# Sparse attention and an MLP on one core: the first batch's prologue rewritten (masks as a bias matmul, local q and k on the upper partitions, filler products)

## The chip, the cores and the metric

The kernel runs on one core of a Trainium2 chip. The metric is the device time of one launch in microseconds; lower is better. A core has five engines with a queue of instructions each: PE (TensorE, matmuls and transposes), DVE (VectorE), ACT (ScalarE), POOL (GpSimd) and SP (SyncE, which here only issues transfers). Transfers issued by SP and ACT go through hardware queues (q1 and q10 in the profile), those issued by POOL through a software queue (q0); all run on the same 16 DMA engines.

## The reference

```python
def _attn_ref(q, k, v):                    # (8, 8, 576, 64) float32 each
    scores = matmul(q, k.transpose(0, 1, 3, 2)) / sqrt(64)
    rel = pos[:, None] - pos[None, :]
    mask_local = (rel >= 0) & (rel < 32)                                  # heads 0 to 3
    mask_strided = (rel >= 0) & (pos[None, :] % 32 == pos[:, None] % 32)  # heads 4 to 7
    scores = where(mask, scores, -1e9)
    return matmul(softmax(scores), v)

def reference(q, k, v, moe_w_in, moe_w_out):
    x = attn_out.transpose(0, 2, 1, 3).reshape(4608, 512)
    h = x @ w_in                            # (512, 2048)
    return (h * tanh(softplus(h))) @ w_out  # (2048, 512)
```

## The kernel before

The work is cut into the 8 batches of the attention (576 tokens each) and 9 tiles of 512 tokens of the MLP. While the MLP runs on tile t, the attention of batch t+1 is woven between its matmuls, and the loads of batch t+2 and later are issued. The order on every engine is the order in which the program issues instructions (a manual schedule); waits are set where an instruction needs another engine's or a transfer's result, or a buffer that is still read.

Attention works on two kinds of heads. For the local heads ("l"), six windows of 96 queries look at 128 keys each. For the strided heads ("s"), the tokens are regrouped so that a unit is a block of 72 queries and 72 keys. `qk` makes products of qT and kT into one of three accumulators in PSUM (`acc(0..2)`, two banks each) and lets ACT write the exponential to `P_s` or `P_l`. `mask` multiplies these by a matrix of zeros and ones on DVE (L289). `pv` and `pv2` multiply by v, with a column of ones that gives the sum, and DVE divides (L316, L317, or L330, L331 for two windows at once). `xt` transposes the result into `xT`, which the MLP reads. qT and kT come from PE transposes with the identity `ident` for batches 0 and 1, and from DMA transposes for batches 2 and later (L172 for s, L180 for l), which SP issues after POOL or DVE has cast the loaded float32 to bf16.

The MLP's first half `mlp1` is 8 groups of 8 matmuls of 128x512 (L428), each two columns of 128 of w_in, and ACT applies Mish (L433). For tile 0 the first two groups are split, so that channels 256 to 511 (the s heads) come first. The second half `mlp2` is 16 groups of 4 matmuls (L467), for tile 0 with w_out's quarters in the outer loop; the next batch's attention steps are placed between these groups (`attn_steps`).

Batch 0 has no MLP to be woven into. Its prologue is written out by hand from L483 on:

- SP issues four loads of k and q of the s heads into `st0` (L493), then v of the s and l heads (L115, L126, L129), then batch 1's local k and q (L104).
- POOL clears `P_l` (L504), issues two casting loads of batch 0's local k and q into `lq0` (L506, on partitions 0 to 95 with 6 tokens each), clears rows 64 to 79 of ks and qs of batch 1 (L534), and copies four numbers of vs (`held`, L535): that copy does nothing but hold the loads of w_in behind it (L136, five pieces) until vs is cast. One cast of vl stands between the third and the fourth piece. Then follow the loads of batch 1's ks and qs (L97) and of the first two quarters of w_out (L142).
- DVE casts ks and qs from `st0` in four steps (L151); PE transposes them (L207), ACT and DVE copy the transposes out of PSUM. The three s parts of `qk` follow, then DVE's masks and the cast of vs, then `t_step_loc0` for local k and q (L236), with `pv2` between, and so on up to `xt` of the local heads and the MLP.

After the prologue, a load of a few bytes of w_in (`gate`, L559) stands in SP's queue: it waits for the fifth piece of w_in, and all SP's later loads (batch 1's v, batch 2's k, q and v) stand behind it. In the same way `rest_of_w_out` holds POOL's loads of w_out's second half behind a copy from batch 1's kTl (L579). SP then issues, in this order: v of batch 1, local k and q of batch 2, vs of batch 2, the DMA transposes of ks and qs of batch 2, vl of batch 2, two stores of the output, and four DMA transposes of local k and q of batch 2.

Of the kernel before, what the change touches and what calls it, by code (L numbers as in the profile page):

```python
# [10 lines left out]
F32 = mybir.dt.float32  # L11
# [6 lines left out]
WQ = 96  # L18
CL, PL = 6, 96
SU = 80  # L20
CS, PN = 8, 72
RING = 4


def _consts():

    kk = np.arange(128)[:, None]
    qq = np.arange(WQ)[None, :]
    rel = qq + 32 - kk
    p = np.arange(PN)  # L30
    c = np.zeros((128, 128 + WQ + PN), np.float32)
    c[:, 0:128] = np.eye(128)
    c[:, 128:128 + WQ] = (rel >= 0) & (rel < STRIDE)
    c[:PN, 128 + WQ:] = (p[:, None] % 4 == p[None, :] % 4) & (p[:, None] <= p[None, :])
    return c.astype(ml_dtypes.bfloat16)


# [1 line left out]
def kernel(ctx, tc, q, k, v, moe_w_in, moe_w_out, out):  # L39
# [12 lines left out]
    w_in = const.tile([128, 4, DF], BF16, name="w_in")  # L52
    w_out = const.tile([128, 16, DM], BF16, name="w_out")
    xT = const.tile([128, 4, RT], BF16, name="xT")
    consts = const.tile([128, 128 + WQ + PN], BF16, name="consts_sb")
    ident = consts[:, 0:128]
    loc = consts[:, 128:128 + WQ]
    stm = consts[0:PN, 128 + WQ:128 + WQ + PN]
    vl32 = const.tile([128, 4, NW, D], F32, name="vl32")
    vs32 = const.tile([128, 4, CS, D], F32, name="vs32")  # L60
    ql32 = const.tile([128, 4, CL, D], F32, name="ql32")
# [11 lines left out]
    P_s = [const.tile([PN, 2, n * PN + 56], BF16, name=f"Ps{i}") for i, n in enumerate((6, 6, 4))]  # L73
    P_l = [const.tile([128, 2, n * WQ + 32], BF16, name=f"Pl{i}") for i, n in enumerate((5, 5, 2))]
    gate = const.tile([1, 256], BF16, name="gate")
    held = const.tile([1, 4], BF16, name="held")
    x_l = const.tile([128, NW, 256], BF16, name="x_l")
    x_s = const.tile([128, CS, 256], BF16, name="x_s")

# [7 lines left out]
    def acc(i, name):  # L87

        return ps_a.tile([128, 2, 512], F32, tag=f"acc{i}", name=name)
# [50 lines left out]
    def load_w_out(c0, c1):  # L140
        for c in range(c0, c1):
            nc.gpsimd.dma_start(  # L142
                w_out[:, 4 * c:4 * c + 4, :],
                moe_w_out.rearrange("(fc p) o -> p fc o", p=128)[:, 4 * c:4 * c + 4, :],
            )

    def cast(eng, out_, in_):
        if eng is nc.scalar:
# [82 lines left out]
    def t_step_loc0(src, dst, hp, eng):  # L231

        tr = tile_t("tr")[:].bitcast(BF16)
        for j in range(CL):
            for e in range(2):
                nc.tensor.transpose(  # L236
                    tr[64 * e:64 * e + 64, PL * j:PL * j + PL], src[0:PL, 2 * hp + e, j, :],
                    ident[0:PL, 0:PL],
                )
        cast(  # L240
            eng, dst.rearrange("c (p j) -> c p j", j=CL),
            tr[:, 0:S].rearrange("c (j p) -> c p j", j=CL),
        )

    T_ORDER = [(kd, w, hp) for kd in ("s", "l") for hp in range(2) for w in ("k", "q")]

# [12 lines left out]
    class Attn:  # L259
        def __init__(self, b):  # L260
            self.b = b

        def qk(self, parts, i_acc):

            ps, o = acc(i_acc, "ps"), 0
            todo = []
            for kind, i in parts:
                w = WQ if kind == "l" else PN
                o0 = o
                for x, y in PARTS[kind][i]:  # L270
                    for e in range(2):
                        r = slice(64 * e, 64 * e + 64)
                        if kind == "l":
                            lhsT, rhs = kTl[r, y, WQ * x:WQ * x + 128], qTl[r, y, WQ * x:WQ * x + WQ]
                        else:
                            c0 = SU * (4 * y + x)
                            lhsT, rhs = kTs[r, c0:c0 + 128], qTs[r, c0:c0 + PN]
                        nc.tensor.matmul(ps[:, e, o:o + w], lhsT=lhsT, rhs=rhs, start=True, stop=True)  # L278
                    o += w
                todo.append((kind, i, o0, o - o0))  # L280
            for kind, i, o0, nw in todo:
                n, pt = (128, P_l[i]) if kind == "l" else (PN, P_s[i])
                nc.scalar.activation(pt[0:n, :, 0:nw], ps[0:n, :, o0:o0 + nw], AF.Exp, scale=scale)  # L283
# [199 lines left out]

    with tc.manual_schedule():
        Po, Dv, Sc = nc.gpsimd, nc.vector, nc.scalar
        Sc.preload_act_table(AF.Exp)
        Sc.dma_start(consts[:], consts_h.ap())
        st0 = g_pool.tile([128, 16, 512], BF16, tag="gT", name="st0")
# [9 lines left out]
        load_v_loc(0)  # L498
        load_qk_loc(1)
        lq0 = g_pool.tile([128, 16, 512], BF16, tag="gT", name="lq0")  # L500
        lq0 = lq0[:].rearrange("p a b -> p (a b)")[0:PL]
        kl0, ql0 = [lq0[:, 1536 * i:1536 * i + 1536].rearrange("p (h x) -> p h x", h=4) for i in range(2)]
        for p in P_l:
            Po.memset(p[:], 0.0)  # L504
        for dst, src in ((kl0, k), (ql0, q)):
            Po.dma_start(dst, src[0, 0:4].rearrange("h (p j) d -> p h (j d)", j=CL))  # L506
        kl0, ql0 = [x.rearrange("p h (j d) -> p h j d", d=D) for x in (kl0, ql0)]
        Dv.memset(kTs[:], 0.0)
        Dv.memset(kTl[:, :, 0:32], 0.0)
# [7 lines left out]
            Dv.memset(p[:], 0.0)  # L517

        a = Attn(0)
        for hp in range(2):  # L520
            h = 2 * hp
            cast(Dv, ks[0][0:PN, h:h + 2, :], st0[0][:, h:h + 2, :])
            t_step(0, "s", "k", hp, Sc)
        for hp in range(2):
            h = 2 * hp
            cast(Dv, qs[0][0:PN, h:h + 2, :], st0[1][:, h:h + 2, :])
            t_step(0, "s", "q", hp, Dv if hp else Sc)
        for i in range(3):
            a.qk([("s", i)], i)
        a.mask("s", 0, Dv)  # L530
        cast(Dv, vs[0][0:PN, :, :, 0:D], vs32[0:PN])
        a.mask("s", 1, Dv)
        for x in (ks, qs):
            Po.memset(x[1][64:SU], 0.0)  # L534
        Po.tensor_copy(held[:], vs[0][0:1, 3, 0, 0:4])  # L535
        load_w_in(0, 256)
        load_w_in(256, 512)
        load_w_in(512, 1024)
        cast_v_loc(0, Po, 0, 3)
        load_w_in(1024, 1536)  # L540
        load_w_in(1536, 2048)
        for hp in range(2):
            t_step_loc0(kl0, kTl[:, hp, 32:32 + S], hp, Sc)
        a.pv2("s", 0, 0)
        a.mask("s", 2, Dv)
        a.pv2("s", 2, 1)
        for hp in range(2):
            t_step_loc0(ql0, qTl[:, hp, :], hp, Sc)
        a.qk([("l", 0)], 2)
        a.pv2("s", 4, 0)  # L550
        a.qk([("l", 1)], 1)
        a.mask("l", 0, Dv)
        a.pv2("s", 6, 0)
        cast_v_loc(0, Sc, 3, 6)
        a.qk([("l", 2)], 2)
        a.mask("l", 1, Dv)
        load_qk_str(1)
        load_w_out(0, 2)
        nc.sync.dma_start(gate[:], w_in[0:1, 0, 1536:1792])  # L559
        load_v(1)  # L560
        accs = (2, 1, 0)
        gT, g1 = mlp1(0, accs)
        a.xt("s", 0)
        a.xt("s", 1)
        Sc.preload_act_table(AF.Mish)
        a.pv2("l", 0, 1)
        a.mask("l", 2, Dv)
        a.pv2("l", 2, 0)
        a.pv("l", 4)
        a.pv("l", 5)  # L570
        a.xt("l", 0)
        a.xt("l", 1)
        cast_qk_loc(1, Po, Po)
        for x in (ks, qs):
            Po.memset(x[0][64:SU], 0.0)
        load_qk_loc(2)

        def rest_of_w_out():
            Po.tensor_copy(held[:], kTl[0:1, 1, 32:36])  # L579
            load_w_out(2, 4)  # L580
            load_qk_str(2)
            cast_qk_loc(2, Po, Po)
# [78 lines left out]
```

The softmax here doesn't subtract the row's maximum and nothing guards it: scores larger than these inputs give would overflow.

## Time and profile before

| what | value |
|---|---|
| median of 4 runs | 321.33 us (320.7 to 323.05) |
| the profiled execution | 322.08 us, of which the span is 320.3 us |
| PE, busy in the span | 301.4 us (94%) |
| ACT / DVE / POOL, busy in the span | 172.7 / 128.0 / 42.0 us |
| granted clock of PE, mean | 1.00 |
| bytes moved | 46.72 MB, 146 GB/s over the span |
| mean DMA engine busy share, first slices of 8 us | 6, then 9 (tenths) to about 200 us |
| first MLP matmul (L428) | 26.48 us |
| first matmul with w_out (L467) | 44.12 us |

All times within the profile count from the span's start. The span is from the first to the last instruction of the profiled execution; the time of that execution is 1.8 us longer. A line of the timeline gives the start, the time to the end of the last instruction of a merged group, the engine, the line of the program, the operation and its tiles; in brackets stands how long the engine was idle just before it, and what ended that. A line of the waits gives the engine, the waiting operation, what it waited for, the total in microseconds, how often, and the longest. A line of the chain gives the start, the length and what the end of the program hung on at that time. A line of a queue gives its packets, its megabytes and the time of its packets as a share of 16 engines' time; shares of several queues add up to more than 100% where packets overlap. The duration of a transfer issue on SP is how long SP was held by it, not how long the transfer took.

### The profile page before, as it was taken

Reading aid. Unit: us, or ns where it says so; the run is one execution under the profiler, and the core shown is the slowest. Engines: PE = TensorE matmul, PEld = TensorE weight load, DVE = VectorE, ACT = ScalarE, POOL = GpSimd, SP = SyncE. Lnnn points to the kernel's source line nnn. Section 1 sums busy time; section 2 is a strip of 40 time slices with the busy share of each in tenths; the row PEclk is TensorE's granted clock in tenths of the full one; section 3 lists DMA queues with packets and bytes.
Section 4 is the critical chain, followed back from the end, with each engine's and each line's share of the span. In section 5 each row is a group of like instructions: output and inputs, shape, how many; then the busy total and the mean of one; then the engine's idle time right before and its main releaser. Section 6 shows DMA issues by size and latency. Waiting matters only on the chain.

```text
span 320.3 us, 5867 instructions
## 1 busy us (share of the span) xinstructions
PE 301.4 (94%) x2488; PEld 159.7 (50%) x2488; DVE 128.0 (40%) x332; ACT 172.7 (54%) x195; POOL 42.0 (13%) x50
## 2 busy tenths in 40 slices
PE   0678999899899999999999999999999999999995
PEld 0564455444454445544578555445544554444444
DVE  6672067800477038703880288028801830000000
ACT  2572654386637673757475646664666466315601
POOL 9288030245000100200020000000000000000000
PEclk9999999999999999999999999999999999999999
DMA  6999999999999999899979995895540101011012
GB/s 172 217 229 206 222 203 188 177 194 227 178 185 216 171 189 211 195 140 184 223 140 172 184 207 115 159 197 137 96 100 0 68 22 46 0 65 65 2 56 75
DMA packets 103114, 46.72 MB, mean 146 GB/s; under 512 B 85168, under 2 KB 95728, under 8 KB 103088
## 3 DMA queue, kind: packets, MB, share of 16 engines
q1 hardware_dynamic: 91648, 37.22, 64.3%
q0 software_dynamic: 11152, 8.92, 18.5%
q8 instruction: 19, 0.31, 0.4%
q10 hardware_dynamic: 288, 0.21, 0.2%
q14 instruction: 7, 0.06, 0.1%
HBM read 38.34 MB, written 9.44 MB: 149 GB/s over the span
## 4 chain that ended last, share of the span: by engine, by line
PE 81%; DVE 11%; DMA 4%; ACT 1%; issue 1%; SPq 0%; ACTq 0%
PE psh L428 38%; PE pso L467 28%; PE po L305 4%; PE pso L449 4%; DMA qTl<-ql 3%; PE ps L278 3%; DVE x_l L317 3%; DVE x_s L317 2%; PE trx L344 2%; DVE Pl L289 1%; DVE rden L316 1%; DVE ks L151 1%; DMA st<-in_k_dram 1%; PE trx L354 1%; PE tr L207 1%
## 5 line engine op out<-in xcount | busy, mean ns | idle before, releaser
L428 PE MATMUL psh<-xT,w_in 128*128 128x512 bf16 (+1 forms) x640 | 128.6, 362 | 0.0
L467 PE MATMUL pso<-w_out,gT 128*128 128x512 bf16 x512 | 126.3, 379 | 0.0
L433 ACT ACTIVATE gT<-psh 128x1024 bf16<-128x1024 f32 x72 | 73.6, 1024 | 45.2 <-PE psh L428 44.6
L428 PEld LDWEIGHTS <-w_in 128*128 128x128 bf16 x640 | 63.1, 99 | 63.1 <-issue 3.0
L467 PEld LDWEIGHTS <-gT 128*128 128x128 bf16 x512 | 43.6, 97 | 39.0
L289 DVE TENSOR_TENSOR Ps<-Ps,consts_sb 72x864 bf16<-72x864 bf16 (+1 forms) x24 | 13.2, 551 | 88.8 <-ACT Ps L283 88.8
L149 ACT COPY xT<-trx 128x576 bf16<-128x576 bf16 x32 | 20.2, 640 | 37.6 <-PE trx L354 28.2
L474 ACT COPY osb<-pso 128x1024 f32<-128x1024 f32 x16 | 16.2, 1012 | 22.6 <-PE pso L467 13.8
L283 ACT ACTIVATE Ps<-ps 72x864 bf16<-72x864 f32 (+1 forms) x24 | 18.5, 804 | 14.7 <-PE ps L278 14.7
L316 DVE RECIPROCAL rden<-po 72x4 f32<-72x4 f32 (+1 forms) x100 | 17.4, 174 | 18.4 <-PE po L305 18.3
L317 DVE TENSOR_TENSOR x_s<-po,rden 72x256 bf16<-72x256 f32 x56 | 23.5, 420 | 1.9
L151 DVE COPY osb<-pso 128x512 f32<-128x512 f32 (+1 forms) x2 | 1.1, 558 | 54.5 <-PE pso L449 54.5
L283 ACT ACTIVATE Pl<-ps 128x960 bf16<-128x960 f32 (+1 forms) x24 | 18.7, 806 | 3.6 <-PE ps L278 3.5
L305 PEld LDWEIGHTS <-Ps 72*128 72x128 bf16 x256 | 13.9, 101 | 12.5 <-DVE Ps L289 2.3
L317 DVE TENSOR_TENSOR x_l<-po,rden 96x256 bf16<-96x256 f32 x44 | 18.5, 421 | 1.5
L305 PE MATMUL po<-vs,Ps 72*128 72x65 bf16 x256 | 17.6, 201 | 0.9 <-DVE x_s L331 0.5
L97 POOL DMA_DIRECT2D ks<-in_k_dram x7 | 6.0, 855 | 80.9 <-DMA kTs<-ks 80.9
L305 PE MATMUL po<-vl,Pl 128*128 128x65 bf16 x192 | 12.9, 201 | 2.2 <-DVE x_s L317 0.7
L449 PE MATMUL pso<-w_out,gT 128*128 128x512 bf16 (+1 forms) x80 | 14.0, 337 | 0.0
L289 DVE TENSOR_TENSOR Pl<-Pl,consts_sb 128x960 bf16<-128x960 bf16 (+1 forms) x24 | 13.4, 559 | 0.0
L305 PEld LDWEIGHTS <-Pl 128*128 128x128 bf16 x192 | 9.9, 103 | 6.5 <-DVE x_l L317 1.8
L151 DVE CAST vl<-vl 128x768 bf16<-128x768 f32 x12 | 10.9, 943 | 0.9 <-DMA vl<-in_v_dram 0.9
(70 smaller groups left out, 178.2 us busy)
## 6 DMA issues: line engine op xcount, KB each, us to landing
out_dram<-osb SPq DMA_DIRECT2D x16, 512.0 KB, 3.8
vl<-in_v_dram SPq DMA_DIRECT2D x7, 768.0 KB
vs<-in_v_dram SPq DMA_DIRECT2D x8, 576.0 KB
kl<-in_k_dram SPq DMA_DIRECT2D x7, 576.0 KB, 8.8
ql<-in_q_dram SPq DMA_DIRECT2D x7, 576.0 KB, 9.4
w_out<-in_moe_w_out_dram POOLq DMA_DIRECT2D x4, 512.0 KB, 15.1
ks<-in_k_dram POOLq DMA_DIRECT2D x7, 288.0 KB, 8.1
qs<-in_q_dram POOLq DMA_DIRECT2D x7, 288.0 KB, 9.5
```

Of the source, the lines that this page charges most:

```text
L149: nc.scalar.copy(out_, in_)
L151: eng.tensor_copy(out_, in_)
L283: nc.scalar.activation(pt[0:n, :, 0:nw], ps[0:n, :, o0:o0 + nw], AF.Exp, scale=scale)
L289: meng.tensor_tensor(out=pm, in0=pm, in1=mk[0:n, :].unsqueeze(1).unsqueeze(1).to_broadcast([n, 2, nu, w]), op=ALU.mult,)
L305: nc.tensor.matmul(po[:, h, :], lhsT=pt[0:n, c0:c0 + 128], rhs=rhs, start=True, stop=True,)
L316: nc.vector.reciprocal(rden[0:m, :], po[0:m, :, D])
L317: nc.vector.tensor_tensor(out=dst.rearrange("p (h d) -> p h d", h=4), in0=po[0:m, :, 0:D], in1=rden[0:m, :].unsqueeze(2).to_broadcast([m, ...
L428: nc.tensor.matmul(ps[:, u, o:o + n], lhsT=w_in[:, cc, fc * 128:(fc + 1) * 128], rhs=xT[:, cc, a:a + n], start=(cc == 2), stop=(cc == 1),)
L433: nc.scalar.activation(gT[:, 2 * g:2 * g + 2, :], ps[:], AF.Mish)
L449: nc.tensor.matmul(p, lhsT=gT[:, fc, 128 * ot:128 * ot + 128], rhs=w_out[:, fc, c0:c1], start=(fc == 0), stop=(fc == 15),)
L467: nc.tensor.matmul(p[:, ot % 2, :], lhsT=gT[:, fc, 128 * ot:128 * ot + 128], rhs=w_out[:, fc, :], start=(fc == 0), stop=(fc == 15),)
L474: nc.scalar.copy(osb[:], p[:])
```

## The change

Everything that changes concerns batch 0's prologue.

- The constants grow by two matrices, `locb` and `stmb`, with -30000 where the masks have 0. A new step `bias` writes them into an accumulator with a matmul by the identity, before q and k are there; `qk` then adds its products (`start=False`). Batch 0's six mask steps on DVE go. Later batches keep them.
- Local k and q of batch 0 are loaded on partitions 64 to 127 with 9 tokens each, and are transposed in 18 steps of 64x64 for each pair of heads instead of 12 of 96x64. The first of the four copies goes to DVE.
- A new step `busy` multiplies a tile of zeros by itself, 128 columns at a time: 40 times ahead of the first transposes, 8 times between the first and the second, 8 times before the last s bias.
- POOL clears `P_l` and the rows of ks and qs as four-byte numbers. The clearing of ks and qs of batch 1 moves behind the first load of w_in; `held` now waits for ql0's transfer rather than for vs; both casts of vl go to POOL, ahead of the fourth piece of w_in.
- The order of batch 0's steps is new: both local transposes come ahead of the first `pv2`, vs is cast after the first local copy, four windows of s are done by single `pv`, all of l by `pv2`, and the last copy to `xT` goes to DVE.

```diff
+C0, P0 = 9, 64
...
+    c[:, o:o + WQ] = -30000.0 * (1 - c[:, 128:128 + WQ])
+    c[:PN, o + WQ:] = -30000.0 * (1 - c[:PN, 128 + WQ:o])
...
+    def clear(eng, x):
+        eng.memset(x.bitcast(F32), 0.0)
...
     def t_step_loc0(src, dst, hp, eng):
...
-        for j in range(CL):
+        for j in range(C0):
             for e in range(2):
                 nc.tensor.transpose(
-                    tr[64 * e:64 * e + 64, PL * j:PL * j + PL], src[0:PL, 2 * hp + e, j, :],
-                    ident[0:PL, 0:PL],
+                    tr[64 * e:64 * e + 64, P0 * j:P0 * j + P0], src[:, 2 * hp + e, j, :],
+                    ident[P0:128, P0:128],
                 )
...
+    def busy(n, i_acc):
+
+        ps = acc(i_acc, "ps")
+        for _ in range(n):
+            nc.tensor.matmul(ps[:, 0, 0:128], lhsT=zero[:], rhs=zero[:], start=True, stop=True)
...
+        def bias(self, kind, i, i_acc):
+
+            n, w, mk = (128, WQ, locb) if kind == "l" else (PN, PN, stmb)
+            nu = len(PARTS[kind][i])
+            ps = acc(i_acc, "ps")
+            for e in range(2):
+                nc.tensor.matmul(
+                    ps[:, e, 0:nu * w].rearrange("p (u c) -> p u c", u=nu), lhsT=ident[0:n, :],
+                    rhs=mk.unsqueeze(1).to_broadcast([n, nu, w]), start=True, stop=True,
+                )
+            return ps
...
+        Dv.memset(zero[:], 0.0)
...
         for p in P_l:
-            Po.memset(p[:], 0.0)
+            clear(Po, p[:].rearrange("p e c -> p (e c)"))
         for dst, src in ((kl0, k), (ql0, q)):
-            Po.dma_start(dst, src[0, 0:4].rearrange("h (p j) d -> p h (j d)", j=CL))
+            Po.dma_start(dst, src[0, 0:4].rearrange("h (p j) d -> p h (j d)", j=C0))
...
         a = Attn(0)
+        busy(40, 0)
         for hp in range(2):
             h = 2 * hp
             cast(Dv, ks[0][0:PN, h:h + 2, :], st0[0][:, h:h + 2, :])
             t_step(0, "s", "k", hp, Sc)
+            if hp == 0:
+                busy(8, 0)
+        sb = [a.bias("s", i, i) for i in (1, 2)]
+        busy(8, 0)
+        sb.insert(0, a.bias("s", 0, 0))
...
         for i in range(3):
-            a.qk([("s", i)], i)
-        a.mask("s", 0, Dv)
-        cast(Dv, vs[0][0:PN, :, :, 0:D], vs32[0:PN])
-        a.mask("s", 1, Dv)
+            a.qk([("s", i)], i, sb[i])
+        Po.tensor_copy(held[P0:P0 + 1], ql0[0:1, 3, 0, 0:4])
+        load_w_in(0, 256)
         for x in (ks, qs):
-            Po.memset(x[1][64:SU], 0.0)
-        Po.tensor_copy(held[:], vs[0][0:1, 3, 0, 0:4])
-        load_w_in(0, 256)
+            clear(Po, x[1][64:SU].rearrange("p h x -> p (h x)"))
         load_w_in(256, 512)
         load_w_in(512, 1024)
         cast_v_loc(0, Po, 0, 3)
+        cast_v_loc(0, Po, 3, 6)
         load_w_in(1024, 1536)
         load_w_in(1536, 2048)
         for hp in range(2):
-            t_step_loc0(kl0, kTl[:, hp, 32:32 + S], hp, Sc)
-        a.pv2("s", 0, 0)
-        a.mask("s", 2, Dv)
-        a.pv2("s", 2, 1)
+            t_step_loc0(kl0, kTl[:, hp, 32:32 + S], hp, Sc if hp else Dv)
+        cast(Dv, vs[0][0:PN, :, :, 0:D], vs32[0:PN])
+        lb = [a.bias("l", i, i) for i in range(2)]
         for hp in range(2):
             t_step_loc0(ql0, qTl[:, hp, :], hp, Sc)
-        a.qk([("l", 0)], 2)
-        a.pv2("s", 4, 0)
-        a.qk([("l", 1)], 1)
-        a.mask("l", 0, Dv)
-        a.pv2("s", 6, 0)
-        cast_v_loc(0, Sc, 3, 6)
-        a.qk([("l", 2)], 2)
-        a.mask("l", 1, Dv)
+        a.pv2("s", 0, 2)
+        a.qk([("l", 0)], 0, lb[0])
+        a.qk([("l", 1)], 1, lb[1])
+        a.pv("s", 2)
+        a.pv("s", 3)
+        a.pv2("s", 4, 2)
+        a.qk([("l", 2)], 0, a.bias("l", 2, 0))
+        a.pv("s", 6)
+        a.pv("s", 7)
+        a.pv2("l", 0, 1)
...
         gT, g1 = mlp1(0, accs)
+        a.pv2("l", 2, 2)
         a.xt("s", 0)
         a.xt("s", 1)
         Sc.preload_act_table(AF.Mish)
-        a.pv2("l", 0, 1)
-        a.mask("l", 2, Dv)
-        a.pv2("l", 2, 0)
-        a.pv("l", 4)
-        a.pv("l", 5)
+        a.pv2("l", 4, 0)
         a.xt("l", 0)
-        a.xt("l", 1)
+        a.xt("l", 1, Dv)
```

## Prediction, made before the changed kernel was run

> **What bounds the kernel now.** I read the page first: PE is busy 94% of the span and carries 81% of the chain that ended last, yet "DMA qTl<-ql" has a line in that chain. So I asked next for PE's own waits over the whole span, of which these are the longest:
>
> ```profile
> PE tr L207 <- DVE ks L151: 8.5, 2, 6.9
> PE ps L278 <- DMA qTl<-ql: 1.3, 1, 1.3
> PE trx L344 <- DVE x_l L317: 1.0, 1, 1.0
> PE po L305 <- DVE x_s L317: 0.7, 1, 0.7
> ```
>
> All waits of PE but three lie before 26.5 us. Two are batch 1's small ones (the 0.7 at 57 us, a 0.2 at 59). The third is the wait that decides this case, so I read the chain and PE's timeline around it:
>
> ```profile
> 75.97 9.89 DMA qTl<-ql
> 85.90 0.43 PE L278 MATMUL ps<-qTl,kTl 64*128 64x96 bf16 x12 [1.29 <-DMA qTl<-ql]
> ```
>
> At 84.6 us PE has done all it can and waits until 85.9 for the last transposed q of batch 2. From there to 320.3 PE has no further wait for a DMA. A change in the prologue thus has 1.3 us of free gain plus whatever it moves this landing. So what does the landing hang on? SP's own timeline:
>
> ```profile
> 33.70 0.63 SPq L559 DMA_DIRECT2D gate<-w_in  x1
> ...
> 35.59 10.10 SPq L109 DMA_DIRECT2D kl<-in_k_dram  x1
> 45.78 7.77 SPq L109 DMA_DIRECT2D ql<-in_q_dram  x1
> 53.65 5.48 SPq L115 DMA_DIRECT2D vs<-in_v_dram  x1
> 59.23 2.37 SPq L172 DMA_TRANSPOSE kTs<-ks  x1
> 61.70 5.41 SPq L172 DMA_TRANSPOSE qTs<-qs  x1
> ```
>
> Each issue begins where the one before ends, from the gate (33.7, when the last piece of w_in has landed) to 77.7. Between them the 16 engines' share stays above 1.0 with short dips (0.87 in 66 to 68, 0.89 in 76 to 78), and mostly 170 to 250 GB/s move. The stretch is a transfer chain, not one of compute: the compute that it needs (casts of vs by 47.4, PE's last reads of kTl by 55.5, osb by 66.3) is done before each issue. The last link, by queue, from 78 to 82 us:
>
> ```profile
> q0 software_dynamic: 837, 0.64, 106.8%
> q1 hardware_dynamic: 194, 0.04, 9.2%
> ```
>
> POOL's four loads of ks and qs (issued 75.06 to 77.9) hold the engines, and SP's last transpose (75.97 to 77.7) waits behind them.
>
> Last, the start of the MLP on PE's weight loads:
>
> ```profile
> 30.74 0.15 PEld L428 LDWEIGHTS <-w_in 128*128 128x128 bf16 x1 [0.28 <-issue]
> 31.14 0.31 PEld L428 LDWEIGHTS <-w_in 128*128 128x128 bf16 x2 [0.25 <-issue]
> ```
>
> From 26.5 to 31.1 they come 0.427 us apart, 0.216 afterwards: PE runs at half speed until 4.7 us of dense work. (The granted clock reads 1.00 all along and doesn't show it.)
>
> **The change, part by part.** The sums are for the profiled execution: 322.08 us, span 320.3 plus 1.8; that is 0.75 above the median of the runs, 321.33.
>
> *POOL's memsets moved behind the first w_in load.* They run 4.46 to 8.55 now, beside the DVE casts of ks (1.94 and 2.37 us; the like casts of qs, with POOL quiet, 0.67). Without them 1.27 + 1.69 = 3.0 us leave DVE, but the second half of k and both of q may land only by 9.0 and 9.6, where DVE takes them now without a wait. So q is ready between 0 and 3 us earlier; I take 1. Written as four-byte elements, the memsets should take half, 0.9 us each, between w_in's first and second load: issues slip about 1.5 us, but w_in's first load, issued at 15.37, landed only at 23.5, so the queue isn't empty meanwhile: nothing. Were it empty, 1.5 us later.
>
> *Zero products.* 40 + 8 + 8 of 128 columns at 0.107 us (a quarter of 0.427): 4.3 us from about 1.1 to 5.4, ended as the first cast does (4.86 + 0.67), and 1.7 us in the wait for q. Beside waits: nothing; 0.9 us if q comes early.
>
> *Bias matmuls for masks.* Off DVE: 0.60 + 0.60 + 0.45 + 0.65 + 0.65 + 0.35 = 3.3 us. Onto PE: 12 matmuls, 4608 columns, 1.9 us warm, 3.8 cold. Those for s lie in the wait for q, those for l in the wait for lq's second landing.
>
> *Local transposes.* 72 of 64 columns for 48 of 96. 24 took 1.17 us (49 ns each, cold): between -0.4 (warm, 27 ns each as the pairs of batch 1) and +1.2 us; taken 0.
>
> *The order after ql0 lands.* PE now stands in front of ql0's transposes before any pv. That landing is at 14.8 (issue 3.73 + 11.1). Behind it: transposes and first pv about 1.7 us, then DVE: five pairs (0.20 + 0.69 + 0.04) and four singles (0.17 + 0.42 + 0.04), 7.2 us, then the last transposes 0.4. So the MLP starts at about 24.2 for 26.5, and warm, which saves 11 x 0.211 = 2.3 us more: 4.6 us in all; 2.3 if cold.
>
> *What is late next.* w_in's five pieces landed at 23.5, 24.8, 27.4, 29.9 and 33.7: just enough. MLP1 of tile 0 would end at 24.2 + 48 x 0.216 + 4.5 (groups 6, 7 and the transposes between) + 0.5 = 39.6. But w_out's first quarter landed at 22.2 + 19.5 = 41.7, and PE first reads it at 44.1 now. So PE waits 2.1 us and 2.4 us of the lead remain. With them it reaches batch 2's qTl at 82.2, and waits 3.7 us for 85.9. All of the compute gain is gone there.
>
> *What moves the transfers.* The engines have been saturated since about 5 us, so the chain moves only by work saved. lq goes from 768 packets of 1.5 KB to 512 of 2.3 KB. From 11 to 14 us 446 such packets took 70.3% of the 16 engines: 76 ns each. If a packet's price stays: 256 x 76 / 16 = 1.2 us saved; if it grows with its bytes: 0. I take 0.6. lq is issued 1 us earlier (P_l's memset halved) into a stretch at 0.84: 0 to 0.3, taken 0.2. consts grow by 43 KB, at 217 GB/s 0.2 us. POOL's later gate for w_out's second half opens at 38 rather than 42.7, but w_out's first half lands until 45.3, so the queue had work anyway: it swaps order, no bytes. Together -0.6, bounds -1.5 and +0.2.
>
> [...] The row: 0.33 MB of lq in 3 us, 110 GB/s. [...]
>
> **The rivals.** *A, the landing stands (0.48):* PE waits longer for w_out and qTl, the end follows the transfers: 321.33 - 0.6 = 320.7.
>
> *B, the landing gives way (0.33):* SP's transposes slip ahead of POOL's four loads. They miss by little (77.7 against data from 78), and 7 us hang on it; or SP's chain takes less than I think once PE is ahead. Then PE keeps 2.4 + 1.3 = 3.7: 317.6; and if w_out comes earlier too, 4.6 + 1.3 = 5.9: 315.4. For it: the 9.89 us are mostly standing behind others. Against: both queues follow the same landing of vl, so their order is unlikely to move.
>
> [...]
>
> *D, the prologue doesn't speed up or loads come later (0.07):* 321 to 323.
>
> **How the numbers follow.** About 0.5%, 1.6 us, can be told from no change. A gives mostly "same", with a sixth of it beyond -1.6 and little beyond +1.6; B is faster; C is on the edge and beyond; D is half and half. Faster 0.37, same 0.46, slower 0.17. The likeliest case alone: 319.6 to 321.6. The range takes in B's first form and C: 316.8 to 323.1.
>
> **What would show it.** In the profile after: POOL quiet from 4 to 12 us and casts of ks at 0.67; no half-speed stretch at L428; the MLP's first matmul near 24; a PE wait of about 2 us before the first L467 group, for w_out; a wait of 3 to 4 us for qTl, ended near 85.3; afterwards rows at the same distances. Wrong if qTl lands before 83 (B), if L467 after it comes at double spacing (C), or if SP's chain shows gaps that end with compute.

## The result, and the profile after

The changed kernel's median is 323.56 us (36 executions, 319.71 to 327.8), that of the kernel before beside it 321.81 us (55, 319.86 to 329.37); the ratio is 1.0009, 95% interval 0.9988 to 1.003. By the half per cent named in the prediction that is no change. Ratios leave out executions over 1.5% above the fastest of the same kernel, here 14 of the changed kernel's 36 and 4 of the 55 before; as the profiled execution, in which the clock falls, is one of these 14, medians of all executions stand beside the ratios. By these the changed kernel is 1.75 us slower.

The profiled execution took 325.49 us, span 323.7, which is 3.4 us more than the profile of before. PE's waits in it, the longest first (us in all, times, longest one):

```profile
PE ps L309 <- DMA qTl<-ql: 2.9, 1, 2.9
PE ps L309 <- ACT Ps L317: 1.3, 1, 1.3
PE tr L217 <- DVE ks L161: 1.3, 2, 0.9
PE tr L217 <- DVE qs L161: 1.1, 1, 1.1
```

The 8.5 us for ks are down to 1.3, so the prologue did become shorter. The wait for batch 2's last transposed q has grown from 1.3 to 2.9, as the prediction has it, and there is a new one that it does not have, for an exponential on ACT. The MLP on PE's weight loads, and the first matmul that reads w_out:

```profile
24.58 0.22 PEld L462 LDWEIGHTS <-w_in 128*128 128x128 bf16 x2
...
27.21 0.15 PEld L462 LDWEIGHTS <-w_in 128*128 128x128 bf16 x1 [0.28 <-issue]
27.64 0.79 PEld L462 LDWEIGHTS <-w_in 128*128 128x128 bf16 x4 [0.28 <-issue]
```

```profile
41.53 1.03 PE L501 MATMUL pso<-w_out,gT 128*128 128x512 bf16 x4
```

The MLP starts 1.8 us earlier (24.58 for 26.40 on the weight loads), and 7 of its matmuls come at half speed where 11 did. The second need not be the change's doing: in experiment 1, which has the prologue of before, 7 come at half speed as well, and full speed is there at 29.39 where before has it at 31.14:

```profile
26.39 0.22 PEld L428 LDWEIGHTS <-w_in 128*128 128x128 bf16 x2
...
29.39 1.61 PEld L428 LDWEIGHTS <-w_in 128*128 128x128 bf16 x8 [0.22 <-issue]
```

At 41.53, where before stands at 44.12 and experiment 1 at 43.23, PE has a lead of 2.6 us over before, 1.7 over experiment 1, and it did not wait for w_out. The new wait comes next. ACT's rows, and PE's row behind them:

```profile
44.34 1.28 ACT L317 ACT_TABLE_LOAD   x1 [2.10 <-PE ps L309]
45.63 0.89 ACT L317 ACTIVATE Ps<-ps 72x864 bf16<-72x864 f32 x1
```

```profile
46.57 0.37 PE L309 MATMUL ps<-qTs,kTs 64*128 64x72 bf16 x12 [1.35 <-ACT Ps L317]
```

ACT sits idle for 2.10 us until PE's scores are there, and only then loads the table of the exponential. In before the same load stood ahead of that wait, in ACT's idle time:

```profile
44.84 1.28 ACT L283 ACT_TABLE_LOAD   x1
46.88 0.89 ACT L283 ACTIVATE Ps<-ps 72x864 bf16<-72x864 f32 x1 [0.76 <-PE ps L278]
```

So 1.35 of the 2.6 us are gone. With the other 1.26 PE reaches the q (idle from 83.35; before from 84.61):

```profile
86.27 0.67 PE L309 MATMUL ps<-qTl,kTl 64*128 64x96 bf16 x12 [2.92 <-DMA qTl<-ql]
...
92.70 0.39 PE L309 MATMUL ps<-qTl,kTl 64*128 64x96 bf16 x10
```

The wait closes as a sum: 1.29 of before + 1.26 of lead + 0.37 by which the q lands later = 2.92. The stretches around it (PE, PEld, DVE, ACT and POOL busy with counts, granted clock, DMA share, GB/s) show what the wait cost besides:

```profile
84.00:85.00 1.00, 0.00 (x0) 0.00 (x0) 0.00 (x0) 0.00 (x0) 0.00 (x0) 1.00 1.48 154
85.00:86.00 1.00, 0.00 (x0) 0.00 (x0) 0.00 (x0) 0.00 (x0) 0.00 (x0) 0.88 1.27 156
86.00:87.00 1.00, 0.73 (x15) 0.59 (x15) 0.00 (x0) 0.43 (x1) 0.00 (x0) 0.50 1.30 170
88.00:89.00 1.00, 1.00 (x7) 0.45 (x6) 0.00 (x0) 0.45 (x1) 0.00 (x0) 0.50 1.33 176
```

The granted clock falls to 0.50 within the wait and stays there to 92.6. The next group of the kind (x10) follows 6.43 us after the first; in before it followed after 3.43 (85.90, 89.33). That is 3.0 us lost, and 3.0 + 0.37 is the whole difference of the spans.

In the trace's record of the clock the fall is at 85.75 and the rise at 92.58, and all its changes lie whole multiples of 3.413 us apart: the stretches between them are 6.83, 17.07, 58.03 and 6.83 us long, which is 2, 5, 17 and 2 times half of the shortest. In before the record's two changes, at 31.10 and 321.23, lie 290.13 us apart, 85 times 3.413. In the last 3.413 us ahead of the fall PE worked for 1.00 us. In before the piece that holds the wait, counted from 31.10 in steps of 3.413, has 2.31 us of work, and the clock stayed up:

```profile
82.34:85.75 3.41, 1.00 (x14) 0.35 (x13) 1.19 (x5) 0.00 (x0) 0.00 (x0) 1.00 1.52 121
```

```profile
82.30:85.71 3.41, 2.31 (x26) 0.99 (x25) 2.23 (x6) 0.83 (x2) 0.00 (x0) 1.00 1.29 170
```

So the moment of the fall does not go by the length of the wait alone: in experiment 5 it comes 2.0 us after PE's last matmul, here 2.4. On the page the fall is the pair of sevens in the middle of the clock's row; the low digits at its start are the prologue, which the record has at half speed from 10.7 to 27.7 us (before's row shows nines there, although its MLP starts at half speed too):

```profile
PEclk9657999999779999999999999999999999999999
```

### The profile page after: what moved, and what is told of

Its sections match the earlier page's. It is cut to its first block, busy times and chain, and to the rows that moved or that the text cites. A ratio compares the mean times of both kernels' runs of the same rounds, so it can differ in the third digit from the quotient of the medians.

```text
span 323.7 us, 6055 instructions
## 1 busy us (share of the span) xinstructions
PE 309.7 (96%) x2580; PEld 165.3 (51%) x2580; DVE 123.7 (38%) x331; ACT 170.8 (53%) x192; POOL 36.1 (11%) x51
## 4 chain that ended last, share of the span: by engine, by line
PE 80%; DMA 8%; DVE 8%; SPq 1%; issue 1%; ACT 1%; POOL 0%; DVEq 0%; ACTq 0%; POOLq 0%
PE psh L462 38%; PE pso L501 28%; DMA vl<-in_v_dram 5%; PE pso L483 4%; PE po L339 4%; DMA qTl<-ql 3%; PE ps L309 3%; DVE x_l L351 2%; DVE x_s L351 2%; PE trx L378 1%; DVE rden L350 1%; DVE Pl L323 1%; PE trx L388 1%; DVE vl L161 1%; SPq L528 0%
## 5 line engine op out<-in xcount | busy, mean ns | idle before, releaser
L501 PE MATMUL pso<-w_out,gT 128*128 128x512 bf16 x512 | 129.0, 385 | 0.0
L467 ACT ACTIVATE gT<-psh 128x1024 bf16<-128x1024 f32 x72 | 73.5, 1024 | 43.8 <-PE psh L462 43.4
L501 PEld LDWEIGHTS <-gT 128*128 128x128 bf16 x512 | 44.1, 99 | 39.9 <-issue 1.7
L323 DVE TENSOR_TENSOR Ps<-Ps,consts_sb 72x864 bf16<-72x864 bf16 (+1 forms) x21 | 11.6, 551 | 89.7 <-ACT Ps L317 89.7
L351 DVE TENSOR_TENSOR x_s<-po,rden 72x256 bf16<-72x256 f32 x60 | 25.2, 420 | 2.1
L339 PEld LDWEIGHTS <-Ps 72*128 72x128 bf16 x256 | 14.3, 103 | 12.1 <-DVE Ps L323 2.6
L351 DVE TENSOR_TENSOR x_l<-po,rden 96x256 bf16<-96x256 f32 x42 | 17.7, 421 | 1.4
L339 PE MATMUL po<-vs,Ps 72*128 72x65 bf16 x256 | 18.0, 203 | 0.0
L339 PE MATMUL po<-vl,Pl 128*128 128x65 bf16 x192 | 13.0, 201 | 2.2 <-DVE x_s L351 0.7
L104 POOL DMA_DIRECT2D ks<-in_k_dram x7 | 5.2, 746 | 84.5 <-DMA kTs<-ks 84.5
L339 PEld LDWEIGHTS <-Pl 128*128 128x128 bf16 x192 | 10.1, 102 | 6.4 <-DVE x_l L351 1.8
L323 DVE TENSOR_TENSOR Pl<-Pl,consts_sb 128x960 bf16<-128x960 bf16 (+1 forms) x21 | 11.5, 545 | 0.0
L483 PEld LDWEIGHTS <-gT 128*128 128x128 bf16 x80 | 7.8, 98 | 6.2
```

Source lines behind the costliest of these rows:

```text
L323: meng.tensor_tensor(out=pm, in0=pm, in1=mk[0:n, :].unsqueeze(1).unsqueeze(1).to_broadcast([n, 2, nu, w]), op=ALU.mult,)
L339: nc.tensor.matmul(po[:, h, :], lhsT=pt[0:n, c0:c0 + 128], rhs=rhs, start=True, stop=True,)
L351: nc.vector.tensor_tensor(out=dst.rearrange("p (h d) -> p h d", h=4), in0=po[0:m, :, 0:D], in1=rden[0:m, :].unsqueeze(2).to_broadcast([m, ...
L467: nc.scalar.activation(gT[:, 2 * g:2 * g + 2, :], ps[:], AF.Mish)
L483: nc.tensor.matmul(p, lhsT=gT[:, fc, 128 * ot:128 * ot + 128], rhs=w_out[:, fc, c0:c1], start=(fc == 0), stop=(fc == 15),)
L501: nc.tensor.matmul(p[:, ot % 2, :], lhsT=gT[:, fc, 128 * ot:128 * ot + 128], rhs=w_out[:, fc, :], start=(fc == 0), stop=(fc == 15),)
```

## Experiments

Two theories stood against each other. The first: the end hangs on the landing of batch 2's q, so prologue gain ends in that wait, and a wait of some 3 us also costs the clock. The rival: some other place takes the gain, first of all another transfer, that of batch 1's v.

**1. The kernel before, with POOL's four loads held until the last q has landed.**

```diff
+                    if t == 1:
+                        Po.tensor_copy(held[0:1], qTl[0:1, 1, 0:4])
                     for b in range(max(3, t + 2 + (t > 1)), min(t + 4, B)):
```

> The kernel before with one addition: POOL's four loads of ks and qs of batches 3 and 4 are held behind the last transposed q of batch 2. Theory of the landing (PE waits for that q, and the q stands behind POOL's loads): the q lands near 79 instead of 85.9, PE's wait of 1.29 us goes, the time falls by 1.3 us to about 320.4 (ratio 0.996). Rival (the q is late for another reason, such as the slow transpose itself, or the chain of SP's own loads): the landing stays within 1 us of 85.9 and the ratio is 1.000.

Measured: median 320.74, ratio 0.9973 (0.995 to 0.9996). The held copy, which follows the q, and PE's group:

```profile
78.39 0.18 POOL L625 COPY held<-qTl 1x4 bf16<-1x4 bf16 x1 [4.23 <-DMA qTl<-ql]
```

```profile
83.49 0.46 PE L278 MATMUL ps<-qTl,kTl 64*128 64x96 bf16 x14
```

The q lands by 78.4 for 85.90 and PE no longer stops there. That POOL's loads hold up SP's transposes is thereby shown. How much of the 1.3 us is kept is not: the ratio leaves 0.1 to 1.6 us, and PE, which the fewer half-speed matmuls put 0.9 us further ahead, has a new wait one batch later, for batch 3's last q. Before has none there.

```profile
117.13 0.43 PE L278 MATMUL ps<-qTl,kTl 64*128 64x96 bf16 x12 [0.94 <-DMA qTl<-ql]
```

**2. The same hold in the changed kernel.**

> The changed kernel with the same hold. Theory of the landing: PE's wait for the q (2.92 us) and the stretch at half speed behind it (86.3 to 92.7 us, worth about 3.0 us against the rows of before) both go; the profiled execution falls from 325.5 to about 319.5, the median to 318.5 to 319.5, ratio to before 0.990 to 0.993. Rival (the prologue's lead is lost elsewhere and the wait only shows it): another wait of 2 to 3 us appears behind 86 us, the ratio stays at 0.998 to 1.002.

Measured: median 322.76, ratio 1.000 (0.9964 to 1.0036): nothing gained. The q is in time (landed by 77.7), but PE stops before. DVE's first cast of batch 1's v, then PE's waits from 44 us on:

```profile
55.96 0.95 DVE L161 CAST vl<-vl 128x768 bf16<-128x768 f32 x1 [3.43 <-DMA vl<-in_v_dram]
```

```profile
PE po L339 <- DVE x_s L351: 3.9, 2, 2.9
PE ps L309 <- ACT Ps L317: 1.3, 1, 1.3
```

The clock then reads 0.50 from 58 to 64. The first theory alone falls: there is a second place, some 28 us earlier.

**3. The changed kernel with 45 products of zeros where PE waits for the q.**

```diff
-            [Q(x, *sl2), Q(y, l0), V("s", 2)],
+            ([lambda: busy(45, x)] if b == 2 else []) + [Q(x, *sl2), Q(y, l0), V("s", 2)],
```

> The changed kernel with 45 products of zeros (128 columns, about 2.5 us) on PE just ahead of the products that wait for batch 2's q. Nothing is added to the result. Theory that the long wait costs PE its speed: the wait for the q shrinks from 2.9 to about 0.4 us, the landing stays near 86, the granted clock stays at 1.00 behind it, and the execution falls by 3 us to about 322.5; the median to 321.5 to 322 (ratio 1.000). Rival (the drop of the clock comes from something else, such as the prologue's own pattern or power): the clock falls all the same, the time stays at 323.5 or rises.

Measured: in the profiled execution 323.25 us, 2.2 below the changed kernel's.

```profile
83.16 2.67 PE L259 MATMUL ps<-zero 128*128 128x128 bf16 x45
...
87.08 0.43 PE L309 MATMUL ps<-qTl,kTl 64*128 64x96 bf16 x12 [0.85 <-DMA qTl<-ql]
90.51 0.39 PE L309 MATMUL ps<-qTl,kTl 64*128 64x96 bf16 x10
```

The q lands even later (87.08), yet the clock stays at 1.00 and the next group follows after 3.43 us, as in before: the 3.0 us are the clock's. But the median is 326.89, ratio 1.0055 (1.0025 to 1.0084), where 1.000 was expected: 9 executions lie at 322.5 to 323.6, 10 at 326.9 to 330.7. Which wait those ten met no profile shows; the late v with the fill on top of it would fit.

**4. The changed kernel without its products of zeros.** 

```diff
-        busy(40, 0)
...
-            if hp == 0:
-                busy(8, 0)
         sb = [a.bias("s", i, i) for i in (1, 2)]
-        busy(8, 0)
```

> The changed kernel without its 56 products of zeros. Theory of the landing: the MLP starts 0 to 1 us later than 24.7 and its half-speed matmuls are 11 instead of 7, so PE comes to the q 1 to 2 us later and waits 1 to 2 us instead of 2.9; the landing stays near 86; time 321 to 322.5, ratio 0.998 to 1.002, and the clock falls less often behind the wait. Rival (the zero products carry the gain, and without them something is lost): slower by 2 us or more, ratio 1.006 or more.

Measured: median 324.27, ratio 1.0032 (1.0006 to 1.0057). The MLP starts 0.2 us later (24.81 on the weight loads), and again 7 of its matmuls are at half speed:

```profile
24.81 0.22 PEld L462 LDWEIGHTS <-w_in 128*128 128x128 bf16 x2
...
27.81 2.26 PEld L462 LDWEIGHTS <-w_in 128*128 128x128 bf16 x11 [0.22 <-issue]
```

With the products in place the same start lies anywhere from 24.07 (experiment 2) to 25.45 (experiment 6), so no gain of theirs is seen here. The profile also has the late v, a DVE wait of 5.14 us for it ended at 58.06, so the ratio is not their price.

**5. The changed kernel with w_out's second half issued later.**

```diff
-            Po.tensor_copy(held[0:1], kTl[0:1, 1, 32:36])
+            Po.tensor_copy(held[0:1], kTs[0:1, 0:4])
...
-                    if i == 8:
+                    if i == 9:
                         rest_of_w_out()
```

> The changed kernel; POOL's loads of w_out's second half and of batch 2's ks and qs are held behind batch 1's first copy to kTs instead of the one to kTl, so they are issued near 42.2 us instead of 40.5. Two-place theory (PE's lead is lost at batch 1's vl when those loads get ahead of it, which the runs show where they were issued 5.4 us or less after vl, and otherwise at batch 2's q; each wait past 3 us costs another 3 us of half speed): vl is in time (cast near 52.7, no wait), PE's first wait for a transfer is the q's, about 2.9 us near 86; the highest runs (above 326) go; median 322 to 323, ratio 0.999 to 1.003. Rival (only the q matters): times as the changed kernel's, up to 328.

Measured: median 325.19, ratio 1.0034 (1.0002 to 1.0067). The v was in time (cast at 52.54, no wait), and the lead now arrives at the q, with a wait of 2.84 us and half speed behind it; 14 of 22 executions lie above 324.6. That is slower than the expected 322 to 323, and two executions are still above 326. In the profiles, taking one of the two places away moves the loss to the other.

**6, 7. Both holds, in the changed kernel and in the kernel before.** The edits of 1 and 5 together.

> The changed kernel with both holds: the later gate for w_out's second half, and POOL's loads of batches 3 and 4 behind batch 2's last transposed q. Two-place theory: PE waits for neither transfer, its lead of 1.3 us and the former wait of 1.3 us are kept and the clock stays at 1.00 after the MLP's start; span 317.5 to 318.3, time about 319.5, ratio 0.990 to 0.994, and runs within 2 us of each other. Rival (a third place takes the lead): a new wait of 2 us or more on PE behind 44 us, ratio 0.998 or more.

> The kernel before with both holds. Two-place theory: what the q costs before is 1.3 us, and vl is in time anyway, so it comes to 320.3 to 320.7, ratio 0.995 to 0.998, near the first run of the kernel before with one hold. The difference to the changed kernel with both holds is then what the change's prologue is worth when nothing takes its lead: 1 to 2 us. Rival (the holds help both alike because transfers go better, not because of waits): the changed kernel with both holds is no faster than this one.

Measured: the changed kernel 321.61, ratio 0.9972 (0.9942 to 1.0002); the kernel before 321.61, ratio 0.9947 (0.9915 to 0.998). In the profile of the first (span 318.4) PE has no wait for a transfer behind 44 us and the clock stays at 1.00 from 29 us on. But the change is worth nothing even then: the expected 0.990 to 0.994 is missed. Its MLP starts 0.9 us earlier (25.45 for 26.39 in experiment 1, on the weight loads), and the table load takes 1.35 again at 47.34. The two close as a sum: PE comes to batch 2's q at 83.92, 0.4 us later than in experiment 1 (83.49). Some executions of both still reach 325; the profile of 7 (324.89) is one of them, and shows where its time went:

```profile
23.69 3.59 DVE L289 TENSOR_TENSOR Pl<-Pl,consts_sb 128x384 bf16<-128x384 bf16 x1
```

```profile
24.18 1.49 POOL L151 CAST kl<-kl 96x1536 bf16<-96x1536 f32 x1
25.59 1.47 POOL L151 CAST ql<-ql 96x1536 bf16<-96x1536 f32 x1
```

The same mask takes 0.35 us in before, where it also starts at 23.69 and POOL's casts at 24.50. Here it ends at 27.3, 0.2 us after the second cast, and the MLP starts near 29.7. That the casts hold it up is likely but not shown: by these rows the mask starts 0.5 us ahead of the first cast.

**8. The kernel before, with w_out's second half issued earlier.**

```diff
-            Po.tensor_copy(held[:], kTl[0:1, 1, 32:36])
+            Po.tensor_copy(held[:], gT[0:1, 8, 0:4])
...
-                    if i == 8:
+                    if i == 6:
                         rest_of_w_out()
```

> The kernel before; POOL's loads of w_out's second half are held behind the fifth result of the MLP's first tile (gT), so they are issued near 39 us, 3.9 us after vl's load instead of 7.8. Nothing else moves. Two-place theory: they get ahead of batch 1's vl, whose cast waits until 56 to 59 us, PE idles 3 to 5 us and runs at half speed afterwards; slower by 3 to 6 us, ratio 1.010 to 1.018. Rival (the late vl of the other runs has to do with the changed prologue, such as its order of POOL's and SP's first loads): vl in time, ratio 0.998 to 1.002.

Measured: median 325.1, ratio 1.0081 (1.0059 to 1.0102), less than the expected 1.010 to 1.018, with

```profile
58.85 0.96 DVE L151 CAST vl<-vl 128x768 bf16<-128x768 f32 x1 [5.71 <-DMA vl<-in_v_dram]
```

and a PE wait of 5.2 us behind it. With nothing of the change in it, the kernel before gets the late v from that one issue. The loads concerned: SP issues the v's at 34.89, POOL w_out's second half at 38.01. That distance is 3.1 us here, and 5.4 and 5.1 in the other two profiles with the late v (experiments 2 and 4). In the profiles where the v is in time it is 7.8 (before), 5.9 (after) and 5.5 to 7.0 (1, 3, 5, 6). The 5.9 is close to the edge, but so is experiment 1's 5.6, and that kernel issues these loads as before does. Nor does the distance decide alone: 5.44 was late (2), 5.48 in time (3). How much nearer the change brings the late v is not shown.

**9. The kernel before with both holds, and of the change only POOL's part.**

```diff
-            Po.memset(p[:], 0.0)
+            clear(Po, p[:].rearrange("p e c -> p (e c)"))
...
-        for x in (ks, qs):
-            Po.memset(x[1][64:SU], 0.0)
         Po.tensor_copy(held[:], vs[0][0:1, 3, 0, 0:4])
         load_w_in(0, 256)
+        for x in (ks, qs):
+            clear(Po, x[1][64:SU].rearrange("p h x -> p (h x)"))
```

> The kernel before with both POOL holds, and of the change only its POOL part: the pads cleared as 4-byte zeros (0.95 us for one of ks and qs in place of 1.80), and the clearing of ks and qs taken from ahead of the first casts to behind the first w_in issue. If POOL's memsets are what held the prologue in before, ks is cast in 0.7 us, the first MLP matmul stands at 25.5 to 26.0 us (26.5 before) and the ratio to before is 0.991 to 0.994. If the prologue's length is set by PE's order at half clock and by the landing of local q, the MLP still starts within 0.3 us of 26.5 and the ratio is that of both holds alone, 0.995 to 0.997.

Measured: median 319.97, ratio 0.9936 (0.9913 to 0.996): the fastest version of this study, and faster than both kernels. The first cast of ks takes 0.69 us (1.94 in before), yet the MLP starts at 26.11, 0.3 us earlier: the start is as the second theory has it, the ratio as the first. Its twelve executions lie close together (318.86 to 321.32), where experiment 7 reached 325.37; its interval overlaps that of 7, so what POOL's part adds to the holds is not told apart.

**10. The changed kernel with both holds, and batch 0's masks on DVE again.**

```diff
-        sb = [a.bias("s", i, i) for i in (1, 2)]
-        sb.insert(0, a.bias("s", 0, 0))
...
-            a.qk([("s", i)], i, sb[i])
+            a.qk([("s", i)], i)
+        for i in range(3):
+            a.mask("s", i, Dv)
```

and the like for the local ones.

> The changed kernel with both holds, and batch 0's masks as DVE products again in place of the bias matmuls. If the masks lie on the prologue's path, the local ones (0.65 + 0.65 + 0.35 us on DVE) move the first MLP matmul 1.0 to 2.0 us later, to 26.5 to 27.5, and the ratio against before rises by 0.003 to 0.006 over that of both holds with the bias (0.997), to 1.000 to 1.003. If PE's half speed sets the stage and the masks lie beside it, the bias matmuls (some 3.8 us at half speed) are saved instead and the MLP starts 0.5 to 2 us earlier.

Measured: median 320.93, ratio 0.9958 (0.9935 to 0.998). The MLP starts 0.4 us later than in 6 (25.89 for 25.45), less than the changed kernel's own starts differ, and neither theory gave the rest: the table load is back ahead of its wait, and PE's wait of 1.35 us is gone.

```profile
43.44 1.28 ACT L317 ACT_TABLE_LOAD   x1
45.48 0.89 ACT L317 ACTIVATE Ps<-ps 72x864 bf16<-72x864 f32 x1 [0.76 <-PE ps L309]
```

This separates the masks from all else in the change. The way from PE's first w_out matmul to batch 2's q says the same (start of the x14 or x2 group less start of the first w_out matmul): 41.61 to 41.62 us in after, 6, 11 and 12, which have the bias; 40.26 to 40.28 in before, 1, 9 and 10, which have not. The reason can be read in the waits that the two built programs give to these instructions (Ps is the exponential, and the brackets name the engines waited for):

```
after:  19 LoadActFuncSet [PE]   20 Activation Ps [Activation]   21 Activation Ps [PE, Activation]
masks:  19 LoadActFuncSet [DVE]  20 Activation Ps [PE]           21 Activation Ps [DVE, PE]
```

In both, an exponential that waits for two things leaves one of them on the table load ahead of it. With a DVE mask in batch 0, one of the two is that mask, long done, and it goes to the table load; the bias takes the mask away, and PE's scores go there instead. The traces agree: right ahead of the load ACT waits on PE's semaphore in after (to 44.3 us), and on DVE's in before (43.8) and in experiment 10 (42.4).

What PE gains by this does not reach the end. It comes to batch 2's q at 82.99, 0.9 us ahead of experiment 6, and then waits 0.93 us for batch 3's q at 116.83, as in experiments 1 (0.94), 9 (0.71) and 11 (0.43). Behind the two known places lies a third.

**11. The changed kernel with both holds, and 40 more products of zeros in the prologue.** Twenty of them write into the PSUM bank that holds the third short group's bias, so this kernel's scores of that group in batch 0 are not the reference's.

```diff
+            if hp:
+                for _ in range(20):
+                    nc.tensor.matmul(
+                        sb[2][:, 0, 288:416], lhsT=zero[:], rhs=zero[:], start=True, stop=True
+                    )
...
+        busy(20, 2)
```

> The changed kernel with both holds, and 40 more products of zeros in the prologue: 20 ahead of the second round of local q transposes and 20 behind the local bias matmuls, so that PE has work through 10 to 16 us. If the clock falls at 10.8 us because PE stands idle there, it stays at 1.00 up to the MLP, whose first 7 half-speed products (0.43 us each for 0.22) go, and the first MLP matmul stands at 24.0 to 24.7: 1.5 to 2.5 us in all, ratio 0.989 to 0.993. If the clock falls whatever fills PE, the added products lie on its path at half speed (0.13 us each, up to 2.6 us a block) and the MLP starts 0.5 to 3 us later, ratio 1.000 to 1.006.

Measured: median 321.19, ratio 0.997 (0.9948 to 0.9991). The clock did stay up, but to 22 us only:

```profile
20.00:22.00 2.00, 0.23 (x8) 0.23 (x8) 1.34 (x5) 0.14 (x1) 1.90 (x4) 1.00 1.11 231
22.00:24.00 2.00, 1.78 (x36) 1.69 (x33) 1.69 (x4) 0.57 (x2) 2.00 (x4) 0.56 1.43 197
```

In 20 to 22 PE has a wait of 1.9 us for POOL's half of v (`PE po L339 <- POOL vl L206`), and the clock falls behind it; the MLP starts at 25.64, no earlier than in 6, and at half speed. Here the warmer prologue only runs into that wait. In this profile local q also came 1.4 us later than in 6 (POOL's copy behind it at 15.68 for 14.32), so the gain of warmth by itself stays open.

**12. The changed kernel with both holds, and local q and k on partitions 0 to 95.** 

```diff
-        lq0 = lq0[:].rearrange("p a b -> p (a b)")[P0:128]
+        lq0 = lq0[:].rearrange("p a b -> p (a b)")[0:PL]
...
-            Po.dma_start(dst, src[0, 0:4].rearrange("h (p j) d -> p h (j d)", j=C0))
+            Po.dma_start(dst, src[0, 0:4].rearrange("h (p j) d -> p h (j d)", j=CL))
```

The transposes and their copies go back to 6 tokens too.

> The changed kernel with both holds, and batch 0's local q and k as 6 tokens on partitions 0 to 95, as in the kernel before (768 packets in place of 512). If fewer and longer packets brought the landing forward, local q lands 0.5 to 0.8 us later (near 14.7 where the changed kernel has 14.0), the first MLP matmul 0.3 to 0.8 us later, and the ratio is 0.998 to 1.000. If the landing is set by the time of issue and by the bytes, it stays within 0.3 us, and so do the MLP's start and the ratio (0.997).

Measured: median 321.52, ratio 0.9975 (0.9943 to 1.0006), the same as 6. In the profile local q lands 1.7 us later (POOL's copy at 16.03 for 14.32) and the MLP starts at 26.77 for 25.45. But with one layout that copy stands anywhere from 14.02 (experiment 5) to 15.68 (experiment 11), so one profile does not settle it. No profile shows the 64 partitions to be slower.

## Why the prediction was right, and where it was wrong

The outcome, no change, came by the ratio, and the mechanism of the case on which it was put, A, held: in the profiled execution the gain in the prologue ends in the wait for batch 2's q. Experiment 1 shows that the wait is real, 2 and 6 that the q's landing and PE's lead can be moved apart. But by the prediction's own sign, double spacing behind that wait, the profiled execution is the case that it calls C. Step by step:

- **POOL's memsets.** Right: casts of ks 0.69 us, memsets 0.95, and their new place costs nothing. That they shorten the prologue by 1 us did not hold: 0.3 in experiment 9.
- **Zero products, "nothing".** Held as far as one profile can tell: 0.2 us of the MLP's start, within the spread, and as many half-speed matmuls without them (experiment 4).
- **Start of the MLP, 24.2 and warm.** It was 24.58 and cold: 4 of the 11 half-speed matmuls went, 0.8 us for 2.3 us, and the kernel before has only 7 of them too in experiments 1 and 8, so even this need not be the change's.
- **A wait of 2.1 us for w_out at 41.7.** There was none. w_out's first quarter landed 13.7 us after its issue (at 38.0), not 19.5, and PE came later. That the lead was nonetheless 2.6 us for the 2.4 forecast is luck: a wait that did not come stood against a start that was later and colder than forecast.
- **Masks as bias, hidden.** This step failed. In batch 0 they cost nothing that one profile shows (the MLP starts 0.4 us earlier with the bias, within the spread). But a mask on DVE was also what the table load of batch 1's exponential waited for, and without it the load costs 1.35 us on PE's path. The lead at the q was 1.26, not 2.4; over experiment 1 it is 0.35 (83.14 for 83.49).
- **"It swaps order, no bytes".** This failed too, in some executions: POOL's w_out can get ahead of the v that SP issued before it (experiments 2, 4, 8). Then a wait of 3 to 5 us comes at 55 us and not at 84. In the profile of the changed kernel itself, which issues that w_out 2.3 us earlier than before, the v was in time.
- **Transfers, -0.6.** The q landed 0.37 later in the profile, not 0.6 earlier.
- **C, double spacing behind the wait for the q.** This is what the profile shows. A wait of 2.92 us was enough where the prediction has one of 3.7 (2.84 in experiment 5), and it cost 3.0 us. The range reaches up to 323.1 for C; no run shows from which length on a wait costs the clock: it fell at 2.92 us here and at 1.9 in experiment 11, and stayed up at the 1.29 of before. 14 of 36 executions lie above 324.6, and nine of these have a mean granted clock of 0.963, that of the profiled one, which none of the other 22 has. Which wait they met is not told by it: in experiment 2, where the v was the late one, an execution of 327.09 has 0.963 as well.

When the clock fell, the rows tell more closely. In the changed kernel, with PE's last matmul ended at 83.35, the mean of 0.88 over 85 to 86 puts the fall near 85.8, 2.4 us later; in experiment 5 it came 2.0 us after the last matmul (83.17; mean of 0.65 over 84 to 88). The 3.41 us before a fall need not be idle throughout: PE was busy for 1.00 of them, in experiment 5 for about 1.4. Nor does full speed come a fixed time after the MLP's start: on the weight loads it came after 2.2 us (experiment 9) to 5.1 us (12).

So 320.7 lies close to 1.0009 times the 321.33 it was made for, 321.6, for a sound reason and by luck. Sound is that in A the end follows the q's landing, so the missed steps on the MLP's start, w_out and the masks do not enter the time. The two that do enter, +0.37 for -0.6 at the landing and 3.0 for nothing at the clock, have one sign and do not cancel: they are the 3.4 us of the profiled execution. That the outcome still fits is luck: by the ratio the change costs 0.3 us, by the medians 1.75, a little more than the 1.6 us that the prediction can tell from no change.

What stays open: what the executions near 325 of experiment 6 met; why the late v comes in some executions and not in others at the same distance of issues; and the obvious next kernel, experiment 6 or 9 with the bias and with the table load put ahead of its wait, which wasn't tried. By experiments 9 and 10 it would meet the wait for batch 3's q.

## What to carry to other kernels

Before you count a gain, follow it to the next two or three transfers that another queue can overtake: in the changed kernel each hold alone moved the loss to the other place, and with both some of it went to a third, one batch later (waits of 0.43 to 0.93 us for batch 3's q in experiments 10 and 11). When an operation is taken off an engine, ask also who waited for it; a wait that was long over can be what kept a table load of 1.28 us out of the path. And where PE waits about 3 us, cost the wait with half speed after it, since the shorter prologue here paid 3.0 us for 2.9 us of waiting.

## What the runs showed of the hardware that was not expected

- A 2.9 us wait took the clock to 0.50 for 6.8 us, at a cost of 3.0 us; 2.67 us of zero products with 0.85 us of waiting behind them did not (experiment 3). In the traces of both kernels the clock changes at times that lie whole multiples of 3.413 us apart (2, 5, 17 and 2 times in the changed kernel, 85 times in before), and by the clock's means the half-speed stretches of experiments 2 (57.7 to 64.6) and 4 (58.5 to 65.3) are 6.8 us long as well. That would fit that the same prologue starts its MLP with 7 half-speed matmuls in one execution and 11 in another (experiment 1 and before).
- A DVE product of two SBUF inputs took 3.59 us for 0.35 beside two POOL casts (experiment 7). The product ends 0.2 us after the second cast, but it is recorded as started 0.5 us before the first (23.69 and 24.18), so these rows do not show that the casts held it up.
- The page's granted clock reads 1.00 through the prologue of before and of experiment 9, although their MLPs start with matmuls at twice the price: the record begins with the first stretch at full speed (31.1 us in before).
